# Storing the leftover tokens of a linear-attention and SwiGLU kernel: one transfer of 128 rows in place of two of 64

## The chip, the cores and the metric

The kernel runs on one core of a Trainium2 chip. The metric is the device time of one execution in microseconds (us); lower is better. Times are medians of several runs. The profile is that of one execution.

## The reference

Attention over 32 memory slots per head is followed by a SwiGLU block. Batch is 8, with 8 heads, 576 tokens and a head size of 64; the model width is 512 and the inner width 1536.

```python
a    = softmax(phi, axis=2)                   # over the 576 tokens
k_m  = einsum('bhsm,bhsd->bhmd', a, k)        # 32 slots of 64
v_m  = einsum('bhsm,bhsd->bhmd', a, v)
attn = softmax(q @ k_m.T / 8)
x    = (attn @ v_m) as 4608 rows of 512       # row = batch * 576 + token
out  = (silu(x @ w_gate) * (x @ w_val)) @ w_out   # float32, 4608 x 512
```

## The kernel before

The order of all work is written out by hand. A loop at L996 goes over the batches 2 to 7; batches 0 and 1 are done ahead of it. Each batch `b` has a stage in which TensorE makes gate and value products (`gv_slot`, L545; matmuls at L515) into PSUM banks `p_g` and `p_v`; ScalarE applies SiLU (L532) and VectorE multiplies (L538) into the hidden tile `t_h`.

The last product, with `w_out`, is one level of a Strassen-like scheme of seven block products (`products`, L689). One matmul of it is recorded at L727, into the banks `p_oa`, `p_oc` and `p_os`. Its blocks are 256 tokens by 256 columns, so of the 576 tokens of a batch 512 go through it batch by batch, and 64 are left over. The leftover tokens of four batches are gathered into tiles `t_x` (`ends`, L591), and make a product of their own: batches 0 to 3 in `quad` 0, which runs beside the stage of batch 4 (L1059), and batches 4 to 7 in `quad` 1, which is the last work of the kernel (L1061, L1089). In a quad, one block of rows is 128 rows: the 64 leftover tokens of each of two batches.

The seven products of a batch or quad use banks and intermediate tiles in turn. `keep` (L748) has ScalarE copy a bank into the tile `p1`, `q6` or `p5` (recorded as `t_p`, `t_q`, `t_p` at L752). Each of these tags has one buffer, so the next `keep` of the same tag waits until everything that reads the old tile is done. The four output blocks of a quad are finished by `leftover` (L785), in the order c11, c22, c12, c21 by the printed list of products:

- c11 adds into a tile of the tag `to` (three buffers), recorded as `t_o`;
- c22 adds into the right half of the `p5` tile (`room`), recorded as `t_p`;
- c12 adds into the right half of the `q6` tile, and c21 copies into its left half, both recorded as `t_q`.

Each is then stored to the output by `store_leftover` (L685, DMA issues at L687) in two transfers of 64 rows of 256 columns, one for each batch. In quad 0 both are issued by SyncE (SP). In quad 1 (`end`) the second is issued by ScalarE (ACT), but for c11, whose transfers are both on SP. The full blocks of a batch are stored by `store_block` (L678, issues at L683) on SP. SP also issues the DMA transposes of `t_qT` (L117) and, from batch 4 on, of `t_kT` (`kv_T`, L284). SP's transfers run on the queue q1, ACT's on q10; GpSimd (POOL) issues the loads of q, phi, k and v (`loads`, L982), which run on the queue q0. Those for batch 7 are issued in the stage of batch 4, just behind the leftovers of quad 0.

The order within `products` is the list at its end:

```python
        if quad is not None or b + 1 == B:
            return first + six + five + seven + three + four, ops
        return first + five + six + three + seven + four, ops
```

In it `six` ends in `keep("q6")`, and `seven` goes on accumulating in the bank that this copy reads.

Of the kernel before, what the change touches and what calls it, by code (L numbers as in the profile page):

```python
# [14 lines left out]
def kernel(  # L15
# [19 lines left out]
    nc = tc.nc  # L35
# [3 lines left out]
    B, H, S, D = q.shape  # L39
# [24 lines left out]
    out_b = out.rearrange("(b t) c -> b t c", b=B)  # L64
# [16 lines left out]
    def done(*tiles):  # L81

        for t in tiles:
            free.append(held.pop(id(t))[0])
# [250 lines left out]
    def copy(eng, out, in_):  # L335
        if eng == "a":
            nc.scalar.copy(out=out, in_=in_)  # L337
        else:
            nc.vector.tensor_copy(out=out, in_=in_)
# [345 lines left out]
    def store_leftover(t_o, b, cols, eng):  # L685

        eng.dma_start(out=out_b[b, 512:S, cols], in_=t_o)  # L687

    def products(b, by_hand, quad=None):  # L689
# [5 lines left out]
        end = quad == 1 or (quad is None and b + 1 == B)  # L695
# [87 lines left out]
            both("o2", 256, slice(0, DM))  # L783

        def leftover(name, room, half, cols):  # L785
            engs = (nc.sync, nc.scalar if end and name != "c11" else nc.sync)

            def run():
                if room:
                    t = mine[room, "all"][:, half]  # L790
                else:
                    t = work.tile([128, h], FP32, tag="to", name="t_o")
                home = mine[dict(c11="a", c12="c").get(name, "s")]
                other = dict(c11="p1", c22="p5", c12="q6").get(name)
                if other:
                    nc.vector.tensor_tensor(
                        out=t, in0=home[:, 0], in1=mine[other][:, 0], op=ALU.add
                    )
                else:
                    copy("v" if end else "a", t, home[:, 0])  # L800
                if name != "c22":
                    done(home)
                for k in range(2):
                    x = 4 * quad + 2 * (name > "c20") + k
                    store_leftover(t[64 * k:64 * k + 64], x, cols, engs[k])

            return run

# [2 lines left out]
            c11=c11, c22=c22, c12=c12, c21=c21,  # L811
        )
        if quad is not None:
            ops.update(
                c11=leftover("c11", None, 0, lo), c12=leftover("c12", "q6", 1, hi),
                c22=leftover("c22", "p5", 1, hi), c21=leftover("c21", "q6", 0, lo),
            )
# [178 lines left out]
    for b in range(2, B):  # L996
# [60 lines left out]
        quad = []  # L1057
        if b == 4:
            quad = products(b, (), 0)[0]  # L1059
# [58 lines left out]
```

## Time and profile before

| | before |
|---|---|
| median of 3 runs | 233.5 us (233.14 to 233.53) |
| span of the profiled execution, first to last instruction | 231.4 us |
| median less this span | 2.1 us |
| busy share of TensorE, VectorE, ScalarE, GpSimd | 96%, 80%, 74%, 61% |
| transfers issued at L687 | 16 of 64 KB: 13 on SP, 3 on ACT |
| their time from issue to landing, median | 2.0 us |
| time from the last of them issued (228.28 us) to the end of the span | 3.1 us |

The profile gives no time of its own for its execution beside the span; the 2.1 us are what the median holds beyond it. A line of the timeline has the start in us, the duration in us, the engine, the line of the kernel, the operation and its tiles; a line of one engine with a count above 1 covers a run of such instructions from the first start to the last end. SPq and ACTq mark the issuing of a transfer, which ends long before its data are there. In a table of DMA queues the columns are packets, MB and the time that the packets took, as a share of the time of 16 engines over the stretch asked for.

### The profile page before, as it was taken

To read this page: it belongs to the slowest core of one execution; us is meant where nothing else is said; L and a number is where in the kernel's file an instruction comes from. 1 tells how busy PE (TensorE), PEld (TensorE's weight loads), DVE (VectorE), ACT (ScalarE), POOL (GpSimd) and SP (SyncE) were. 2 spreads that over 40 slices of the span, in tenths; PEclk is the share of its full clock that TensorE was granted. 3 is DMA by queue.
4 is the path that set the end of the run, shared out by engine and by line. 5 is a ranking of instruction groups with operands and counts; after the bars stand their busy time and mean duration, and the time that the engine had idled before them with its cause. 6 is when DMAs were issued, how large, how long until landed. Compare 5 with 4: busy or idle time off the path is not lost.

```text
span 231.4 us, 7210 instructions
## 1 busy us (share of the span) xinstructions
PE 221.6 (96%) x2825; PEld 169.8 (73%) x2825; DVE 185.1 (80%) x423; ACT 171.7 (74%) x365; POOL 140.8 (61%) x190
## 2 busy tenths in 40 slices
PE   6987799999999999999999999999999999999993
PEld 2544476778887777878788787887788778878882
DVE  4245789999966799989997668998999899977732
ACT  2777898988447989968896658978898789677310
POOL 8422427998199049765977689464845394039291
PEclk9999999999999999999999999999999999999998
DMA  6999999999996992999299946994014502202125
GB/s 214 210 211 206 199 207 207 221 245 268 205 225 175 256 256 49 223 204 184 71 223 191 226 134 115 252 236 89 28 65 114 104 0 95 91 10 84 31 85 160
DMA packets 36674, 36.84 MB, mean 159 GB/s; under 512 B 14624, under 2 KB 31008, under 8 KB 36640
## 3 DMA queue, kind: packets, MB, share of 16 engines
q0 software_dynamic: 16272, 22.42, 52.5%
q1 hardware_dynamic: 19600, 13.18, 22.9%
q10 hardware_dynamic: 768, 0.79, 1.1%
q8 instruction: 22, 0.36, 0.6%
q14 instruction: 12, 0.10, 0.1%
HBM read 42.47 MB, written 9.44 MB: 224 GB/s over the span
## 4 chain that ended last, share of the span: by engine, by line
PE 86%; DMA 9%; POOL 2%; ACT 1%; issue 0%; DVE 0%; POOLq 0%
PE p_g L515 21%; PE p_os L727 21%; PE p_v L515 20%; PE p_oc L727 10%; DMA W<-in_moe_w_val_dram 9%; PE p_oa L727 5%; PE p_u L472 5%; PE p_kv L230 2%; PE p_g L396 1%; POOL t_kv L99 1%; POOL t_kv L103 1%; PE p_q L383 0%; POOL t_q L108 0%; ACT t_qT L337 0%; POOL W L138 0%
## 5 line engine op out<-in xcount | busy, mean ns | idle before, releaser
L538 DVE TENSOR_TENSOR t_h<-t_sg,p_v 128x288 bf16<-128x288 bf16 x192 | 81.8, 451 | 14.1 <-PE p_v L515 7.0
L515 PEld LDWEIGHTS <-t_U 128*128 128x128 bf16 x768 | 73.9, 98 | 21.2 <-issue 3.5
L532 ACT ACTIVATE t_sg<-p_g 128x288 bf16<-128x288 f32 x192 | 73.3, 424 | 17.1 <-PE p_g L515 11.4
L515 PE MATMUL p_g<-t_A,t_U 128*128 128x288 bf16 x384 | 77.0, 286 | 0.0
L515 PE MATMUL p_v<-t_A,t_U 128*128 128x288 bf16 x384 | 77.0, 286 | 0.0
L727 PEld LDWEIGHTS <-t_S 128*128 128x128 bf16 x384 | 37.5, 98 | 4.5 <-issue 0.2
L603 POOL TENSOR_TENSOR t_S<-t_h 128x512 bf16<-128x512 bf16 x17 | 19.7, 1157 | 32.7 <-DVE t_h L538 31.2
L727 PEld LDWEIGHTS <-t_h 128*128 128x128 bf16 x288 | 27.1, 98 | 8.6 <-issue 5.0
L492 ACT CAST t_U<-p_u 128x512 bf16<-128x512 f32 x51 | 27.0, 605 | 6.6 <-PE p_u L472 6.6
L727 PE MATMUL p_os<-t_T,t_S 128*128 128x256 bf16 x192 | 23.7, 273 | 0.0
L560 POOL TENSOR_TENSOR t_S<-t_S,t_h 128x512 bf16<-128x512 bf16 x17 | 19.6, 1156 | 1.3
L560 POOL TENSOR_TENSOR t_S<-t_h 128x512 bf16<-128x512 bf16 x16 | 18.4, 1152 | 0.0
L560 POOL TENSOR_TENSOR t_S<-t_h,t_S 128x512 bf16<-128x512 bf16 x16 | 18.4, 1152 | 0.0
L472 PE MATMUL p_u<-W,t_kT 64*32 64x512 bf16 (+1 forms) x416 | 15.3, 363 | 1.2 <-DMA W<-in_moe_w_gate_dram 0.6
L496 DVE CAST t_U<-p_u 128x512 bf16<-128x512 f32 x21 | 13.6, 683 | 1.9 <-PE p_u L472 1.9
L727 PE MATMUL p_os<-t_T,t_h 128*128 128x256 bf16 x96 | 14.8, 273 | 0.0
L875 PE MATMUL p_warm<-bones 128*128 128x512 bf16 x44 | 12.5, 421 | 1.7 <-DVE bones L897 1.7
L452 DVE TENSOR_TENSOR t_A<-t_E,t_lz 128x576 bf16<-128x576 bf16 x16 | 11.4, 740 | 0.7 <-ACT t_lz L428 0.7
L727 PE MATMUL p_oc<-t_T,t_S 128*128 128x256 bf16 x96 | 11.9, 273 | 0.0
L727 PE MATMUL p_oa<-WO,t_h 128*128 128x256 bf16 x96 | 11.8, 273 | 0.0
L727 PE MATMUL p_oc<-WO,t_S 128*128 128x256 bf16 x96 | 11.8, 272 | 0.1
L727 PE MATMUL p_os<-WO,t_h 128*128 128x256 bf16 x96 | 11.8, 273 | 0.0
(107 smaller groups left out, 308.3 us busy)
## 6 DMA issues: line engine op xcount, KB each, us to landing
out_dram<-t_o SPq DMA_DIRECT2D x11, 512.0 KB, 3.0
t_kv<-in_k_dram POOLq DMA_DIRECT2D x8, 576.0 KB, 10.5
t_q<-in_q_dram POOLq DMA_DIRECT2D x8, 576.0 KB, 8.4
t_kv<-in_v_dram POOLq DMA_DIRECT2D x8, 576.0 KB, 14.7
t_phi<-in_phi_dram POOLq DMA_DIRECT2D x6, 576.0 KB, 8.1
out_dram<-t_o SPq DMA_DIRECT2D x10, 256.0 KB, 4.5
WO<-in_moe_w_out_dram POOLq DMA_DIRECT2D x3, 512.0 KB, 19.2
W<-in_moe_w_gate_dram POOLq DMA_DIRECT2D x2, 512.0 KB, 16.5
```

Of the source, the lines that this page charges most:

```text
L230: nc.tensor.matmul(p[g][32 * i:32 * i + 32, 0:n], lhsT=phi_of(b, g, j, i), rhs=kvs[b][64 * g:64 * g + 64, w0:w1, i, j * D:(j + 1) * D], st ...
L452: nc.vector.tensor_tensor(out=a, in0=es.pop((b, g)), in1=lzs.pop((b, g)), op=ALU.mult)
L472: nc.tensor.matmul(p[g][32 * i:32 * i + 32, o:o + n], lhsT=kTs[b][64 * g:64 * g + 64, 2, 32 * i:32 * i + 32], rhs=w_part(w, c, i, g, halve ...
L492: nc.scalar.copy(out=t, in_=p)
L496: nc.vector.tensor_copy(out=t, in_=p)
L515: nc.tensor.matmul(p[:, 0:HALF], lhsT=Us[b, c, g][:, o // 2, which, 128 * (o % 2):128 * (o % 2 + 1)], rhs=atts[b, g][:, r], start=(g == 0) ...
L532: nc.scalar.activation(out=sg, in_=gate[:, 0:HALF], func=AF.Silu)
L538: nc.vector.tensor_tensor(out=dst, in0=sg, in1=val[:, 0:HALF], op=ALU.mult)
L560: eng.tensor_tensor(out=out, in0=x, in1=y, op=ALU.subtract)
L603: eng.tensor_tensor(out=t[:, 0], in0=A21, in1=A22, op=ALU.add)
L727: nc.tensor.matmul(mine[home][:, u], lhsT=lhs(c, m, u), rhs=rhs(c, m), start=fresh and u == 0, stop=(k == 5), skip_group_check=u == 1 or n ...
L875: nc.tensor.matmul(p[:, 0:128 * a], lhsT=bones, rhs=x.to_broadcast([128, a, 128]) if a > 1 else bones, start=True, stop=True,)
```

## The change

For each finished leftover block, the two transfers of 64 rows become one of 128 rows, always issued by SP. On the output side the slice now goes over two batches, then 64 tokens, then 256 columns; on the tile's side it is 128 partitions of 256 elements. In all there are 8 such transfers in place of 16. `store_leftover` is not called any more.

```diff
         def leftover(name, room, half, cols):
-            engs = (nc.sync, nc.scalar if end and name != "c11" else nc.sync)
-
             def run():
...
                 if name != "c22":
                     done(home)
-                for k in range(2):
-                    x = 4 * quad + 2 * (name > "c20") + k
-                    store_leftover(t[64 * k:64 * k + 64], x, cols, engs[k])
+                x = 4 * quad + 2 * (name > "c20")
+                nc.sync.dma_start(out=out_b[x:x + 2, 512:S, cols], in_=t)
 
             return run
```

## The prediction

> **What bounds the kernel now.** I read the page's head first, then the end of the chain of waits, the timeline of the end and of the middle, and last the DMA queues over short stretches.
>
> ```profile
> span 231.4 us, 7210 instructions
> ...
> PE 221.6 (96%) x2825; PEld 169.8 (73%) x2825; DVE 185.1 (80%) x423; ACT 171.7 (74%) x365; POOL 140.8 (61%) x190
> ```
>
> TensorE is the bound almost everywhere: whatever delays it in the middle is added whole to the time. The chain ends otherwise:
>
> ```profile
> 226.88 0.73 PE p_os L727 x6
> 227.61 0.02 issue
> 227.64 0.42 DVE t_q L339
> ```
>
> ```profile
> 228.14 0.47 SPq L687 DMA_DIRECT2D out_dram<-t_q  x1
> 228.28 0.54 ACTq L687 DMA_DIRECT2D out_dram<-t_q  x1
> ```
>
> After TensorE's last product come one copy and the two stores that the change touches. So of the 16 transfers, the last six (c22, c12, c21 of quad 1) stand in the open, issued from 226.76 us on. Their landing takes 1.9 to 2.2 us; from the last issue at 228.28 to the span's end are 3.1 us.
>
> The eight of quad 0 go out between 131.6 and 141.8 us, while TensorE works. But their tile has a second user:
>
> ```profile
> 139.34 2.46 SPq L687 DMA_DIRECT2D out_dram<-t_q  x4
> ...
> 143.66 0.76 POOL L103 DMA_DIRECT2D t_kv<-in_v_dram  x1
> ...
> 150.00 0.58 ACT L752 COPY t_q<-p_os 128x512 f32<-128x512 f32 x1
> ...
> 150.87 1.47 PE L727 MATMUL p_os<-t_T,t_S 128*128 128x256 bf16 x12
> ```
>
> At 150.00 ScalarE writes the one `q6` buffer again, which needs the stores of c12 and c21 to have read it; TensorE goes on in that bank at 150.87. Now these stores have landed by 141.2 + 2.1 = 143.3, so there are 6.7 us to spare.
>
> What a row costs, from the queues over two quiet stretches: 215.1 to 218 (two transfers of 64 rows) and 218.7 to 221 (one of 256 rows of 1 KB):
>
> ```profile
> DMA packets 160, 0.13 MB, mean 45 GB/s; under 512 B 32, under 2 KB 160, under 8 KB 160
> ...
> q1 hardware_dynamic: 160, 0.13, 20.0%
> ```
>
> ```profile
> q1 hardware_dynamic: 272, 0.26, 33.5%
> ```
>
> Each transfer brings 16 packets under 512 B beside its rows, one for each of 16 engines as I read it: 64 rows are dealt out as 4 to an engine. The first gives 0.200 x 16 x 2.9 us / 160 = 58 ns a packet, the second 0.335 x 16 x 2.3 / 272 = 45 ns. The first has few packets in flight, so I use 45 ns, with 40 (2 KB rows in full stretches go at near 390 GB/s, 84 ns, of which half is 42) and 58 as ends.
>
> **The change part by part.**
>
> *Fewer issues.* Eight issues of 0.47 to 0.59 us go. In quad 0 that only shortens SP's queue; nothing on the chain waited for it. At the end ACT's last issue (228.28, landing 2.2 us later, 230.5) goes; SP's alone at 228.14 with the 2.1 us of a 256 KB transfer would land at 230.2. Worth 0.2 us, if all else stays, and it is what is left if the new transfer is spread as the old ones are.
>
> *How the new transfer is cut.* This decides, and no row shows it: all plain transfers of before have a first count of 64 or 128 on both sides. Now the output side counts 2 (batches), 64, 256, and the tile's side 128, 256. The bounds: as now (16 engines, 8 rows each, +0.2 us of data), and not cut at all (one engine, 128 rows). Between them lies a cut along the first count, that is 2 engines with 64 rows each. The rows nearest to it show 64 rows dealt 4 each, equal parts of the first count; with a first count of 2 equal parts of it can be no more than two. The two batches' blocks are not adjacent, so the 128 rows can't be written as one even step. I take 2 engines.
>
> [...]
>
> *The end.* One transfer then holds its two engines for 65 x 45 ns = 2.95 us in place of some 0.2 to 0.5. All three ride SP's one queue, and I take it that they fall on the same engines and go in turn. Data begin 1.1 us after an issue (215.15 to 216.26 in the quiet stretch), so at 226.76 + 1.1 = 227.9; the 512 KB store before them is through by about 227.4. Three in turn end at 227.9 + 8.85 = 236.7. Now the last data are seen at 230.0 and the span ends 1.4 us later: new span 238.1, **+6.7 us** (40 ns: +5.7; 58 ns: +9.2).
>
> *Quad 0.* c22, c12 and c21 begin at 138.14 + 1.1 = 139.25: c22 to 142.2, c12 and c21 to 148.1 if nobody else used the two engines. With 0.4 us from the data's end to landing that is 148.5, 1.5 us ahead of ScalarE's copy: hidden. But the loads for batch 7 have all engines from 143.6 on: POOL's queue fills the stretch 146 to 150 alone, and the last loads end near 153.9. How two queues share shows where stores met loads earlier, in 79 to 81 us:
>
> ```profile
> q0 software_dynamic: 158, 0.29, 63.1%
> q1 hardware_dynamic: 157, 0.29, 42.2%
> ```
>
> One packet for one. In 100 to 103 us a store issued at 100.04 got no packet at all; it landed after 6.9 us in place of some 2.7. By 143.6 c12 has moved about 31 rows; 97 are left on each of the two engines, against some 82 load packets there of 103 to 125 ns (1,310 of queue q0 from 143.6 us on, over 16 engines). In turns the last rows come out behind the last load, and no time is idle: 153.9 + 97 x 45 ns = 158.3, landing at 158.7. ScalarE's copy would start 8.7 us late, and TensorE, which has only 150.87 less 150.58 = 0.3 us to spare and nothing ahead of that product in its order, stops for **8.4 us**. Behind the copy on ScalarE stand the table load and the SiLUs of batch 5; all of it moves by as much, as one shift. Ends: 0 (rows served first) and 8.7. I take the 8.4, since 79 to 81 us is the nearest row.
>
> *c11 of quad 0 and the `t_kT` transpose.* c11's rows hold the two engines from 132.7 to 135.6; the 512 KB store and the transpose behind them on SP come later there by about 1.3 us, so the transpose lands at 140.2 in place of 139.0. Its first reader is TensorE at 140.64. Cost 0, hidden by that 0.4 us; with 58 ns rows it is 0.5, 1 at most.
>
> *Nothing else.* c11 of quad 1 (215.15) is through by 219.2, when the store after it begins; the loads of batch 7 end later but are not read in that stage.
>
> Sum: 231.4 + 6.7 + 8.4 = 246.5 of span; with the 2.1 us by which the median exceeds the span, **248.6 us**.
>
> **The rivals.**
>
> *Spread over 16 as now* (the other side: not slower). Then 8 rows to an engine, +0.2 us of data, less ACT's issue: 233.3, no change; 0.2% of the time, 0.47 us, is about what a measurement of this kernel can tell. For it: 128 rows divide by 16, and every plain transfer in the profile used all 16. It decides if the cut is made along the tile's 128 partitions alone. Chance 0.13.
>
> *Two engines, but the middle is hidden.* If the rows queued by 143.6 keep ahead of the loads, c21 lands by 148.5 to 150 and only the end pays: 233.5 + 6.7 = 240.2 (239.2 to 242.7). For it: c12 and c21 are issued before most of the loads. Against: the 6.9 us landing. Cases in which the loads get fewer turns lie between, up to 246. Chance 0.27.
>
> *Not cut at all.* One engine with 129 packets of 45 ns, 5.8 us each: the end pays 227.9 + 17.4 + 1.4 = 246.7, +15.3; quad 0 lands near 167 and costs some 17: 266. Chance 0.04.
>
> **How the numbers follow.** Two engines and a stall at the `q6` copy: 0.56, its own range 244 to 252.5 (stall 5 to 8.7, end 5.7 to 9.2, transpose up to 1). With the hidden-middle case, from 238.5, these hold 0.83, less some tails: range 238.5 to 252.5. Slower by over 0.2%: 0.56 + 0.27 + 0.04, and a little of the spread case, 0.88. That case gives 0.07 to no change and 0.05 to a gain.
>
> **What the profile after would show.** Small packets fall by 14 for each new transfer if two engines carry it (a quiet c11 in quad 1: 128 rows and 2 small packets; spread it would be 16). From issue to landing c11 of quad 1 takes 1.1 + 2.95 + 0.4 = 4.4 us, the last c21 some 9. In the last 8 us the DMA share is a tenth or two with no engine at work. In the middle, ScalarE's `t_q` copy waits for a DMA of `t_q`, and TensorE has a gap of some 8 us near 151. If the landing times stay near 2.1 us, the cut was wrong and all falls; if they are 4 to 9 but the gap is missing, the sharing was wrong; if each row costs far from 45 ns on two lone engines, the end is mis-sized.

## The result, and the profile after

The changed kernel takes 249.06 us (median of 6 runs, 247.40 to 249.62) against 233.51 us (6 runs of before): a ratio of 1.0655, 95% interval 1.0636 to 1.0674. It is slower by 15.6 us. The profiled execution took 249.4 us with a span of 247.6 us, so the comparison of the two spans gives 16.2 us. All readings below are of the spans.

The head of the page after, and of its costliest groups the two with an idle time that is new (before, no wait stood ahead of the first, and ScalarE never waited for a store in the second). The columns of a group are its tiles and shapes, its busy time, the mean ns of one, the idle time ahead of it and what ended that.

```profile
span 247.6 us, 7197 instructions
...
PE 223.8 (90%) x2825; PEld 170.7 (69%) x2825; DVE 185.2 (75%) x423; ACT 171.7 (69%) x365; POOL 140.6 (57%) x190
...
L727 PE MATMUL p_os<-t_T,t_S 128*128 128x256 bf16 x192 | 25.0, 281 | 6.7 <-ACT t_q L752 6.7
...
L752 ACT COPY t_q<-p_os 128x512 f32<-128x512 f32 (+1 forms) x10 | 5.4, 541 | 14.1 <-DMA out_dram<-t_q 7.0
```

TensorE has the same 2825 products and is busy 2.2 us longer, but it now stops for 6.7 us behind one ScalarE copy, and that copy waits 7.0 us for a store of `t_q`.

The end, in the chain and on the queue of SP:

```profile
236.38 0.74 PE p_os L727 x6
237.11 0.03 issue
237.14 0.42 DVE t_q L339
```

```profile
236.26 0.52 SPq L802 DMA_DIRECT2D out_dram<-t_p  x1
...
236.87 1.26 SPq L802 DMA_DIRECT2D out_dram<-t_q  x2
```

This splits the loss. The last copy starts at 237.14 in place of 227.64: 9.5 us were lost before it. From it to the end of the span are 247.6 - 237.14 = 10.46 us in place of 231.4 - 227.64 = 3.76: another 6.7 us.

How many engines carry a transfer is read here from its small packets. First the whole execution before, then the same after, then the stretch after from 238 to 246 us, when nothing but the last stores was moving:

```profile
DMA packets 36674, 36.84 MB, mean 159 GB/s; under 512 B 14624, under 2 KB 31008, under 8 KB 36640
```

```profile
DMA packets 36434, 36.84 MB, mean 149 GB/s; under 512 B 14384, under 2 KB 30768, under 8 KB 36400
```

```profile
DMA packets 356, 0.37 MB, mean 46 GB/s; under 512 B 4, under 2 KB 355, under 8 KB 355
...
q1 hardware_dynamic: 355, 0.36, 13.5%
```

Before there were 14624 packets under 512 B. Taking away 16 transfers with 16 each and adding 8 with 2 each gives 14624 - 256 + 16 = 14384, as counted. In the last stretch 13.5% of 16 engines are busy, which is 2.2 engines, and 46 GB/s over 8 us make 23 GB/s for each of two: 45 ns for a row of 1 KB. The quietest case is c11 of quad 1, issued at 224.65, with its data moving from 225.7 to 229.0. In the last microsecond of that the two engines move 51 GB/s, 40 ns a row; over all 3.3 us, with 65 packets on each engine, it is 51 ns.

The middle, as the chain of waits has it, first before and then after. Behind it stands the granted clock after the stop, that is the share of its full speed at which TensorE was let run (columns: the stretch and its length, busy time and count for TensorE, weight loads, VectorE, ScalarE and GpSimd, then the clock, the DMA share and GB/s):

```profile
151.03 1.31 PE p_os L727 x12
...
155.53 0.73 PE p_kv L230 x72
```

```profile
141.07 16.82 DMA out_dram<-t_q
157.89 0.02 issue
...
157.99 0.59 ACT t_q L752
158.58 0.04 issue
158.63 2.72 PE p_os L727 x12
...
165.02 0.73 PE p_kv L230 x72
```

```profile
158.00:162.40 4.40, 3.77 (x18) 2.55 (x18) 1.38 (x2) 2.33 (x4) 0.00 (x0) 0.52 0.57 155
162.40:165.00 2.60, 2.60 (x30) 1.91 (x35) 2.18 (x5) 2.18 (x6) 0.00 (x0) 1.00 1.00 186
```

The last store of quad 0, issued at 141.07, holds the `q6` tile until 157.89; before, such a store landed in 2.0 us. When TensorE goes on, its product of 12 matmuls takes 2.72 us in place of 1.31: for 4.4 us the granted clock averages 0.52. From the start of that product to the next `p_kv` product are 158.63 to 165.02 = 6.39 us in place of 151.03 to 155.53 = 4.50. So the slow clock costs 1.9 us. With the stop of 6.74 us that leaves 0.86 us of the 9.5, lost before 149 us, most of it in a gap of 0.69 us of TensorE at 135.3 for which the profile names no cause.

### The profile page after: what moved, and what is told of

The parts are those of the page before. It is cut to its first block, busy times and chain, and to the rows that moved or that the text cites. A ratio compares the mean times of both kernels' runs of the same rounds, so it can differ in the third digit from the quotient of the medians.

```text
span 247.6 us, 7197 instructions
## 1 busy us (share of the span) xinstructions
PE 223.8 (90%) x2825; PEld 170.7 (69%) x2825; DVE 185.2 (75%) x423; ACT 171.7 (69%) x365; POOL 140.6 (57%) x190
## 2 busy tenths in 40 slices
DMA packets 36434, 36.84 MB, mean 149 GB/s; under 512 B 14384, under 2 KB 30768, under 8 KB 36400
## 4 chain that ended last, share of the span: by engine, by line
PE 77%; DMA 15%; POOL 2%; ACT 1%; issue 1%; DVE 0%; DVEq 0%; POOLq 0%; ACTq 0%
PE p_g L515 19%; PE p_os L727 19%; PE p_v L515 18%; PE p_oc L727 8%; DMA W<-in_moe_w_val_dram 8%; DMA out_dram<-t_q 7%; PE p_u L472 4%; PE p_oa L727 4%; PE p_kv L230 2%; POOL t_kv L99 1%; POOL t_kv L103 1%; PE p_g L396 1%; PE p_q L383 0%; POOL t_q L108 0%; ACT t_qT L337 0%
## 5 line engine op out<-in xcount | busy, mean ns | idle before, releaser
L727 PEld LDWEIGHTS <-t_S 128*128 128x128 bf16 x384 | 38.0, 99 | 12.0 <-issue 7.1
L727 PE MATMUL p_os<-t_T,t_S 128*128 128x256 bf16 x192 | 25.0, 281 | 6.7 <-ACT t_q L752 6.7
L752 ACT COPY t_q<-p_os 128x512 f32<-128x512 f32 (+1 forms) x10 | 5.4, 541 | 14.1 <-DMA out_dram<-t_q 7.0
L757 DVE TENSOR_TENSOR t_o<-p_oc,t_q 128x512 f32<-128x512 f32 x8 | 5.5, 686 | 9.7 <-ACT t_q L752 5.7
L452 DVE TENSOR_TENSOR t_A<-t_E,t_lz 128x576 bf16<-128x576 bf16 x16 | 11.4, 739 | 0.7 <-ACT t_lz L428 0.7
```

The source lines that it names most:

```text
L452: nc.vector.tensor_tensor(out=a, in0=es.pop((b, g)), in1=lzs.pop((b, g)), op=ALU.mult)
L727: nc.tensor.matmul(mine[home][:, u], lhsT=lhs(c, m, u), rhs=rhs(c, m), start=fresh and u == 0, stop=(k == 5), skip_group_check=u == 1 or n ...
L757: nc.vector.tensor_tensor(out=out, in0=mine[home], in1=mine[other], op=ALU.add)
```

## The experiments

**The two places apart (e1, e2).** In the changed kernel, one transfer of 128 rows in one quad alone, the old form in the other. This is the edit of e1; e2 has `if not end` in place of `if end`:

```diff
-                nc.sync.dma_start(out=out_b[x:x + 2, 512:S, cols], in_=t)
+                if end:
+                    for k in range(2):
+                        store_leftover(t[64 * k:64 * k + 64], x + k, cols, (nc.sync, nc.scalar if end and name != "c11" else nc.sync)[k])
+                else:
+                    nc.sync.dma_start(out=out_b[x:x + 2, 512:S, cols], in_=t)
```

e1_middle_only:

> One transfer of 128 rows in quad 0 alone; quad 1 stores as before. Theory (the new transfer is carried by 2 engines; in the middle its rows hold the q6 tile until 158 us): the middle's part of the loss, 16.2 us less 6.7 at the end, so 233.5 + 9.5 = 243.0, with a wait of ScalarE's t_q copy for the stores of about 7 us. Rival (one transfer of 128 rows is spread as before, and the loss comes from ACT's help missing at the end): 233.5.

Measured: 243.58 us, ratio 1.0431 (1.0403 to 1.0459).

e2_end_only:

> One transfer of 128 rows in quad 1 alone; quad 0 stores as before. Theory: three transfers in turn on 2 engines, 3 x 2.95 us of data, the end pays 6.7 us and the middle nothing: 240.2, with no wait of the t_q copy near 150 us. Rival (the end is lost because what went wrong in the middle delays it): 233.5.

Measured: 240.38 us, ratio 1.0297 (1.0278 to 1.0317). The waits of the `t_q` copy and of TensorE behind it between 125 and 180 us, of e1 first. In e2 that copy waits for TensorE alone, as before:

```profile
ACT t_q L752 <- DMA out_dram<-t_q: 6.7, 1, 6.7
PE p_os L727 <- ACT t_q L752: 6.4, 1, 6.4
```

```profile
ACT t_q L752 <- PE p_os L727: 0.3, 1, 0.3
```

Both rivals fall: each place pays by itself, 10.2 us and 7.0 us over the 233.37 us of before beside them. Together they make 17.2, more than the 15.6 of the whole change. In the profiled runs most of the excess sits where each run was to be as before: e1 takes 4.39 us from its last copy (237.01) to the end in place of 3.76, and e2 reaches its last copy at 228.24 in place of 227.64. Such amounts are within the spread of before itself, whose spans beside these runs go from 231.3 to 232.4; the cause stays open.

**The order of the rows in the tile (e3).** The transfer stays one, on SP, with the same rows of 1 KB; only the leftover rows lie as token, then batch. The code that fills and reads the tile follows; its lines are left out here:

```diff
-            xs[b // 2] = hpool.tile([128, NJF, 2, 64], BF16, tag="xs", name="t_x")
+            xs[b // 2] = hpool.tile([128, NJF, 64, 2], BF16, tag="xs", name="t_x")
...
-                nc.sync.dma_start(out=out_b[x:x + 2, 512:S, cols], in_=t)
+                nc.sync.dma_start(
+                    out=out_b[x:x + 2, 512:S, cols].rearrange("b t c -> t b c"), in_=t
+                )
```

> Still one transfer of 128 rows on SP, the same bytes in rows of the same 1 KB, but the leftover rows lie in the tile as token, then batch, so the output side counts 64 tokens, 2 batches, 256 columns. Theory (the cut goes along the first count of both sides): 64 and 128 give 16 engines again, 16 small packets a transfer, and the time is 233.3, within 0.3 of before. Rival (a transfer of 128 rows of 1 KB in two places, or SP alone, is what is slow): 249.

Measured: 233.02 us (12 runs, 232.86 to 233.65), ratio 0.9985 (0.9971 to 0.9998). The queue in the quiet stretch from 214.9 to 217.8 us, with its one transfer, c11:

```profile
DMA packets 144, 0.13 MB, mean 45 GB/s; under 512 B 16, under 2 KB 144, under 8 KB 144
...
out_dram<-t_o SPq DMA_DIRECT2D x1, 128.0 KB, 2.1
```

128 rows bring 16 small packets again and land in 2.1 us. The number and size of rows, the queue and the number of transfers are those of the changed kernel; the first count of the output side went from 2 to 64, and the whole loss is gone. Against before this version measures 0.35 us less; its interval excludes 1 so barely that the gain stands at the edge of what these runs can tell. GpSimd's gathering copies (L592) now write with a step and take 490 ns in the mean in place of 435; the total shows no cost of it.

**The move to SP alone (e4).** In the kernel of before, two transfers of 64 rows as before, all on SP:

```diff
-            engs = (nc.sync, nc.scalar if end and name != "c11" else nc.sync)
+            engs = (nc.sync, nc.sync)
```

> Two transfers of 64 rows as before, but all on SP: only the move away from ACT is made. Theory: at the end one more issue of 0.5 us stands before the last landing, 233.8. Rival (the loss is the missing second queue): well over 236.

Measured: 235.02 us, ratio 1.0070 (1.0054 to 1.0086). The rival falls, but the cost is 1.65 us and not the 0.5 expected. I had counted the last issue alone, but it stands at the end of a queue of six:

```profile
226.82 1.11 SPq L687 DMA_DIRECT2D out_dram<-t_p  x2
228.04 2.80 SPq L687 DMA_DIRECT2D out_dram<-t_q  x4
```

At some 0.55 us each, with gaps, they follow one another, and the last starts near 230.3 in place of 228.3. So ACT's help at the end was worth 1.65 us, and with all on SP, one transfer in place of two is worth 235.02 - 233.02 = 2.0 us when it is spread over 16 engines.

**A dose between 2 and 16 (e9).** In the changed kernel, a block of 128 rows is 32 tokens of each of four batches. Only the store is shown; the gathering copies change with it, and so does the place of 12 products of quad 1:

```diff
-                x = 4 * quad + 2 * (name > "c20")
-                nc.sync.dma_start(out=out_b[x:x + 2, 512:S, cols], in_=t)
+                x, t0 = 4 * quad, 512 + 32 * (name > "c20")
+                nc.sync.dma_start(out=out_b[x:x + 4, t0:t0 + 32, cols], in_=t)
```

> A dose between 2 and 16: a block of 128 leftover rows is now 32 tokens of each of four batches, so that the output side of the one transfer counts 4, 32, 256. It costs two small copies on GpSimd in place of one, and the first 12 products of quad 1 move to the end of the kernel, 12 x 0.11 = 1.3 us. Theory (the largest number that divides the first counts of both sides): 4 engines, 4 small packets a transfer (32 less in all than with 2 times 8, plus 4 times 8: 14400), 33 x 45 ns = 1.5 us each; the rows of quad 0 are in by 144.5, so no wait of the t_q copy; the end takes 227.9 + 1.3 + 4.5 + 1.4 = 235.1 of span, 237.2. Rival (a cut in two or none, whatever the first count): the stall near 150 stays and the end pays 6.7: 250.

Measured: 235.95 us, ratio 1.0104 (1.0083 to 1.0125), with a span of 234.1 us.

```profile
DMA packets 36450, 36.84 MB, mean 157 GB/s; under 512 B 14400, under 2 KB 30784, under 8 KB 36416
```

These are 14400 small packets, as expected for 4 engines (14624 - 256 + 8 x 4), and there is no wait of a `t_q` copy for a store near 150 us. From 229 to 232 us the stores move 92 GB/s, 23 for each of four engines. From the last copy (227.69) to the end are 6.41 us, so the end pays 2.65 us over before's 3.76, where the expectation had 2.4 beside its 1.3 for the moved products; the steps are 6.7 with 2 engines, 2.65 with 4, and with 16 a gain of 0.3 (e3: 231.1 - 227.61 = 3.49). The 1.3 us was wrong: the last copy starts at 227.69 as against 227.64 before, so the products must have left as much room where they had been.

**One queue or the same engines (e8).** c12 of quad 1 on ACT, in the changed kernel:

```diff
-                nc.sync.dma_start(out=out_b[x:x + 2, 512:S, cols], in_=t)
+                eng = nc.scalar if end and name == "c12" else nc.sync
+                eng.dma_start(out=out_b[x:x + 2, 512:S, cols], in_=t)
```

> The changed kernel, with c12 of quad 1 issued by ACT in place of SP. Theory (all the new transfers fall on the same two engines, whichever queue they come from): the end is as long, 249.1. Rival (they queue up because they share SP's queue): c12 runs beside c22 and c21, 2.9 us less, 246.2.

Measured: 249.88 us, ratio 1.0678 (1.0620 to 1.0737). The queues from 237 to 249 us:

```profile
q1 hardware_dynamic: 395, 0.51, 12.6%
q10 hardware_dynamic: 130, 0.13, 3.1%
```

q10 has 130 packets: 128 rows and 2 small ones. Once the block store ahead of them is through, the rate of both queues together is 48 GB/s in most of the slices and never above 51, as against a mean of 46 of the two engines from 238 to 246 us of the changed kernel. So, by the rate, transfers of the two queues share two engines, and the second queue gains nothing: 249.88 us as against 249.06.

**The wait for the tile (e5).** A buffer of its own for the `q6` tile of quad 0, in the changed kernel:

```diff
-            t = tile_of(name, tag=name, bufs=1)[:, 0:U]
+            t = tile_of(name, tag="q6q" if quad == 0 and name == "q6" else name, bufs=1)[:, 0:U]
```

> The changed kernel, with a buffer of its own for the q6 tile of quad 0, so that ScalarE's copy of batch 4 no longer waits for the stores. Theory: the stall of 6.7 us and the low clock behind it (1.9) go, 249.1 - 8.6 = 240.4, and the wait of the t_q copy is gone while the stores are as slow as before. Rival (TensorE is held by the late loads or the slower SP queue in some other way): 246 to 249.

Measured: 241.22 us, ratio 1.0338 (1.0321 to 1.0354). ScalarE's copy starts without a wait for a store:

```profile
150.42 0.57 ACT L752 COPY t_q<-p_os 128x512 f32<-128x512 f32 x1
```

The time is 0.8 us more than expected, and the profile has another wait of that size:

```profile
PE p_u L472 <- DMA t_kT<-t_bkv: 0.8, 1, 0.8
```

The stores' rows still trickle at 153 us (20 packets of q1 from 152.2 to 153.6 us), and the transposes of `t_qT` and `t_kT` for batch 6 follow them on SP's queue: that of `t_qT` lands after 11.4 us in place of 7.1. That the slow rows cause this wait too is read from the order on the queue; no run tests it alone.

**The loads beside the stores (e6).** The loads for batch 7 one stage later, in the changed kernel:

```diff
         if b > 1 and c == 1:
-            loads(b + 3)
+            if b != 4:
+                loads(b + 3)
...
         z_inv_v(b, 1)
+        if b == 5:
+            loads(7)
```

> The changed kernel, with the loads for batch 7 issued one stage later (beside the z and norm work of batch 5), so that the stores of quad 0 have their two engines to themselves. Theory (a row takes turns with a load packet): c21 is in by 140.1 + 8.85 + 0.4 = 149.4, ahead of the copy at 150.9, and the stall goes: 240.4. Rival (the two engines alone are too slow, whatever else runs): a stall of about 7 us stays, 249.

Measured: 245.78 us, ratio 1.0536 (1.0509 to 1.0562). Neither number. The stall in question is gone, as the theory had it: from 143 us on the two engines move 47 GB/s by themselves until 149, and the copy no longer waits for a store:

```profile
150.39 0.58 ACT L753 COPY t_q<-p_os 128x512 f32<-128x512 f32 x1
```

But the loads now meet the transposes for batch 6:

```profile
PE p_u L472 <- DMA t_kT<-t_bkv: 3.4, 1, 3.4
```

```profile
161.00:167.00 6.00, 3.51 (x29) 1.00 1.25 200
167.00:173.00 6.00, 5.11 (x47) 0.72 0.27 95
```

TensorE (busy time and count, then its clock) stops at 164.5 us, and goes on at 167.9 with a mean clock of 0.72. The loads were put where they do harm of their own; that the stores are so late near 150 us because of the loads is shown by the missing wait, and the total is no measure of it.

**The clock behind the stop (e7).** In the changed kernel, 31 idle products, which add nothing to the output, ahead of the product that waits:

```diff
+    N_WARM = 31
...
+        if b == 4 and quad is None:
+            first_of_seven = seven[0]
+            seven[0] = lambda: (warm(4 * N_WARM), first_of_seven())
```

> The changed kernel, with 31 idle products of 512 columns (0.21 us each, 6.6 us in all) on TensorE ahead of the product that waits for the q6 copy; they add nothing to the output. Theory (the idle time lowers the granted clock, seen as 0.50 in the 3.5 us after the stall): the clock stays at 1.00 and 1.9 us come back, 247.2. Rival (the slow products after the stall have another cause): 249.1 or more.

Measured: 246.85 us, ratio 1.0576 (1.0560 to 1.0592). TensorE at 149 to 161 us (busy time and count, then its clock), and in the chain the product that waited and the next `p_kv`:

```profile
149.00:155.00 6.00, 6.00 (x40) 1.00 1.15 217
155.00:161.00 6.00, 6.00 (x42) 1.00 0.75 158
```

```profile
157.95 1.31 PE p_os L728 x12
...
162.45 0.73 PE p_kv L231 x72
```

The clock stays at 1.00 and the way from the waiting product to the next `p_kv` takes its usual 4.50 us in place of 6.39. That 1.9 us come from the clock is shown. The total moved by 2.2 us, but not from this alone: in this run the copy could start at 155.5, 2.5 us earlier than in the changed kernel, and the idle products ran on for some 1.8 us after it was done.

## Why the prediction was right

248.6 us was predicted and 249.06 measured. The cut in two, the end and the wait for the tile were right; the total is better than the middle's parts.

- *The cut.* Two engines: right, shown by 2 small packets a transfer, by the first count of 64 with 16 packets and by that of 4 with 4. The fall of 14 small packets for each new transfer was counted against a spread transfer of 128 rows; against the two transfers of before it is 32 - 2 = 30, 240 in all. The rates go with it: 46 GB/s with the first count of 2, 92 with 4 (e9) and up to 353 with 64 (c11 of quad 1 in e3), each against 128 on the tile's side. What other counts give, no run shows. In e8 two queues of such transfers made 48 GB/s together, the rate of two engines; no run here shows which engines they were.
- *The end.* 6.7 us predicted, 6.7 measured (65 x 45 ns is 2.93 us and not 2.95, which changes 0.1 us in all). The row price of 45 ns, taken from a full stretch of 16 engines, also held for two alone: 45 ns from 238 to 246 us, with 40 to 51 for c11 of quad 1.
- *The stall at the `q6` copy.* The mechanism was right: e5 and e6 take it away, each in its own way. Its size was 8.4 and is 6.74. The stores were in at 157.9, near the 158.7 predicted, but ScalarE would have been free only at 150.96 and TensorE at 151.9, since both were already 0.9 us late. Luck has a part in the 157.9: the same stores of quad 0 were in at 157.4 in e1, 158.6 in e8 and 155.4 in e7.
- *One packet for one.* Too simple. From 150 to 153 us queue q1 moved 32 packets, 16 on each of its two engines, while q0 moved 465, 29 on each of 16 in the mean; what q0 moved on those two engines no view shows. The limit that was taken, the last rows behind the last load, was nearly reached anyway.
- *"All of it moves by as much, as one shift".* This step failed: behind the stop of 6.74 us the granted clock of TensorE averaged 0.52 for 4.4 us, and a further 1.9 us were lost. No term stood for it. Two runs have shorter waits: in e6 a stop of 3.4 us goes with a mean of 0.72 from 167 to 173 us, and in e5 a wait of 0.8 us with 1.00 from 161 to 167 us. How the clock depends on the length of a stop, no run shows beyond these three.
- *The first part of the middle at 0.* It cost 0.86 us. The `t_kT` transpose of batch 5 was not the cause, since its reader did not wait. A gap like the one of 0.69 us at 135.3 shows in e1 (0.5) and e8 (0.9) and not in e5, e6 or e7, which store in quad 0 in the same way. Its cause stays open.
- *Fewer issues.* The prediction gave them 0.2 us if the transfer is spread over 16 engines; e3, which is that case, measures 0.35. That the second queue at the end was saving 1.65 us (e4) it did not see, because it only asked what both edits do together.

The middle's 8.4 came out as 9.5 by errors that partly cancel: 1.7 too much in the stall, 1.9 and 0.86 not counted. So the span was put 1.1 us too short, at 246.5 in place of 247.6. The 2.1 us that were added for what the median holds beyond the span hide half of that, since by the same working they are 249.06 - 247.6 = 1.5 here. That the total is off by only 0.5 us is luck.

## What to carry to other kernels

Before merging two transfers, look at the first dimension of both sides of the merged one: in this kernel first counts of 2, 4 and 64 gave 2, 4 and 16 engines, and the small packets per transfer in the profile were as many. Where the data lie in the wrong order, change the order in the tile, not the number of transfers: here that took the time from 249.06 us to 233.02 (e3). And ask of every store in the middle who writes its tile next: here a store that took 16.8 us was hidden up to the point where a one-buffer tile was needed again.

## What the runs showed of the hardware that was not expected

- A stop of 6.7 us of TensorE is followed by a granted clock of 0.52 over 4.4 us, 1.9 us in all; idle products in its place keep the clock at 1.00 (e7), and a stop of 3.4 us up to 167.9 us goes with a mean of 0.72 from 167 to 173 us (e6). In e5, behind a wait of 0.8 us, it stays at 1.00.
- Issued one after another on one queue, the last six stores of 64 KB cost 1.65 us more than on two (e4); from the first issue (226.82) to the last (230.3) they follow every 0.7 us in the mean.
- Transfers of the first count 2 from two queues make no more together than two engines give, 48 GB/s (e8).
